# Sigmoid attention and an ELU feed-forward layer: weights by tile of the hidden layer, whole stores, and block sums made earlier

## The chip, the cores and the metric

One core of a Trainium2 chip runs the whole kernel. The metric is the time of one execution on the device, in microseconds (us). Three executions of the kernel before took 1148.48, 1149.53 and 1149.55 us; the median is 1149.53.

## The reference

For 8 batches of 448 tokens and 12 heads of width 64, everything in float32:

```python
scores = q @ k.T / sqrt(64) - log(448)
x = (sigmoid(scores) @ v)            # heads side by side: 3584 tokens x 768
h = x @ w_in                         # 768 -> 2048
g = where(h > 0, h, exp(min(h, 0)) - 1)
out = g @ w_out                      # 2048 -> 768
```

## The kernel before, in words

**Number format.** A float32 operand is scaled by a power of two and split into two float16 parts, a high and a low one. A product is three float16 matmuls (high by high, high by low, low by high). Batches 0 and 1 have their attention in float32 and their first layer from the split parts of `w_in`.

**Batches 2 to 7** compute the first layer by a seven-product scheme on 2 x 2 blocks. Its operands are the four blocks of `w_in` and four sums of them, for each of eight units of two f tiles (an f tile is 128 of the 2048 hidden columns). They are made once, on the chip, by `sums_of_parts` (L340), which is a generator: `make_sums` (L418) asks it for one step. A unit takes seven steps: two that add high and low parts to full numbers (DVE, L394) and store blocks "11" and "12"; one with two block additions (DVE, L352) that stores "22"; one with two more additions and the high half of a sum (ACT, L364); three that make a low half (DVE, L368), store it, and make the next high half. The last low half of a unit falls into the first step of the next. All eight units are 57 steps. The results rest in three rotating buffers of a tile `room` and are written to a DRAM tensor `blend` by POOL's DMA queue (L420, `store_sums`). Blocks that need no new scale (six of the eight units) are written straight from `w_in`'s parts `wi`, each in two DMAs, one for the high and one for the low part; for the other two units ACT rescales them first (L386). `room` uses the same memory as `xh`, the first layer's input of batch 2.

**The weights.** `wi` holds for each unit the parts as (high or low, row tile c, 256 columns): an f tile of one c is a run of 128. Its memory becomes, when a unit's sums are made, the ring of ten blocks that the later batches load from `blend` on SP's queue (`load_block`, L955).

**Order of the work.** The schedule is written by hand: program order is the order on each engine. The first stage follows a list of tokens; 21 of them (`K`) are steps of the sums. Then comes the first layer of batch 1 (`moe1`): behind each of its 16 f tiles `beside_first` (L1489) runs what `order` lists, 15 steps of the sums in all. For each batch b from 2 on, a loop over six pairs of heads (numbered 0 to 5 here) mixes scores and sigmoid of pair n (PE to ACT, L681; ACT L692 and DVE L693 split the result), values of pair n-1 (PE), and matmuls of the second layer of batch b-1 (`fill`, L1115) that keep PE at work. `scale_next` takes the next pair's scales from PE through DVE (L195 and following) to POOL (L591, L594); `split_next` then splits the next pair's q and k with these scales (ACT L620, DVE L623) and its v (ACT L209, DVE L210) and issues the loads of a later pair; `measure_next` starts the maxima of another. In batch 2, sums' steps stand at four or five places of a pair, 20 in all, and one call in pair 4 runs all that are left. Behind pair 5 comes the first layer by blocks (`moe1_blocks`, L969): 28 products of 18 matmuls. Each of the two running sums A and B gets a PSUM bank; `bank` issues one matmul of ones into a new bank, then ACT copies a product into it (L1064, L1074) and later products accumulate there. Behind product n `order_of_blocks` has steps of the next pair; those at 18, 19, 20 and 23 are the four steps of one `split_next`. The last two halves of g are left over (`left_of_g`) and are made beside pair 0 of the next batch, or, behind batch 7, at once.

**The end.** The second layer of batch 7 runs alone: 2 halves of four tiles of tokens (48 matmuls each); the fourth of each half holds 64 tokens of batch 6 and 64 of batch 7 and is written by two DMAs.

Of the kernel before, what the change touches and what calls it, by code (L numbers as in the profile page):

```python
# [10 lines left out]
BF16 = mybir.dt.bfloat16  # L11
# [54 lines left out]
def attention_ffn(  # L66
# [9 lines left out]
    nc = tc.nc  # L76
# [46 lines left out]
    wi = space.rearrange("p (u h c x) -> p u h c x", u=NU, h=2, c=NK)  # L123
# [3 lines left out]
    def part(at, n, dt=F16):  # L127
# [4 lines left out]
        "p (n j c h x) -> p n j c h x", n=RING, j=2, c=HK, h=2  # L132
# [147 lines left out]
    def w_in_parts(u):  # L280
# [28 lines left out]

        def lower():  # L310
# [12 lines left out]
            "E": lambda: nc.scalar.mul(d[:, 0], st["t"], s()),  # L323
# [16 lines left out]
    def sums_of_parts():  # L340
# [4 lines left out]
        full = full.rearrange("p (c x) -> p c x", c=NK)  # L345

        def block(t, x):
            c, f = HK * (x[1] == "2"), P * (x[0] == "2")
            return t[:, c : c + HK, f : f + P]
# [6 lines left out]
        def next_out():  # L356
            nonlocal out
            out += 1
            t = room[:, 4 + out % 3]
            return t, t.rearrange("p (c h x) -> p h c x", c=HK, h=2)  # L360
# [16 lines left out]
        def copy(x, slot):  # L377
            w, j = divmod(u, 2)
            if j or u in ALIKE:
                dst = blend[w, slot].rearrange("p (j c h x) -> p j h c x", j=2, c=HK, h=2)  # L380
                for h in range(2):
                    unsent.append((dst[:, j, h], block(wi[:, NU - 1 - u, h], x)))
                return
            t = next_out()
            for h in range(2):
                nc.scalar.mul(t[1][:, h], block(wi[:, NU - 1 - u, h], x), r)  # L386
            store(t, slot)

        for u in (0, 1, 2, 3, 7, 6, 5, 4):
            r = wt[:, u * WF : u * WF + 1]  # L390
            parts = wi[:, NU - 1 - u]
            for i in range(2):
                c = slice(i * HK, (i + 1) * HK)
                nc.vector.tensor_tensor(full[:, c], parts[:, 0, c], parts[:, 1, c], op=ALU.add)  # L394
# [495 lines left out]
    def moe1_products(b, f):  # L890
# [6 lines left out]
        for c in range(NK):  # L897
            for wj, xj in ((0, 0), (0, 1), (1, 0)):
                nc.tensor.matmul(  # L899
                    ph[:, :S], wi[:, NU - 1 - f // WF, wj, c, f % WF * P :][:, :P], hidden_of(b, c)[:, xj],  # L900
# [54 lines left out]
    def load_block(n):  # L955

        b, i = divmod(n, len(USES))
        if b < B - WHOLE:
            k, w = USES[i]
            nc.sync.dma_start(  # L960
                ring[:, n % RING].rearrange("p j c h x -> p (j c h x)"),
# [3 lines left out]
    def moe1_blocks(b, g, m, behind_first, first, beside):  # L965
# [14 lines left out]
        def bank(k, w):  # L980
# [6 lines left out]
            if name not in sums:  # L987
                t = ps.tile([P, 2, 512], F32, tag="psc", name=f"{name}{b}", bufs=2)
                sums[name] = t[:, 0]
                nc.tensor.matmul(  # L990
                    t[:, 0, :S], ones, xh[:, 0].rearrange("p h x -> p (h x)").bitcast(BF16)[:, :S],
                    start=True, stop=True, skip_group_check=True,
                )
            return sums[name][:, :S]

        def product(k, w):
# [3 lines left out]
            for j in range(2):  # L1000
                n = 0
                for c in range(HK):
                    for wj, xj in ((0, 0), (0, 1), (1, 0)):
                        nc.tensor.matmul(  # L1004
                            to[:, j * HS : (j + 1) * HS], block[:, j, c, wj], rhs(k, c, xj),
# [97 lines left out]
        nc.scalar.activation(warm, bias, AF.Sigmoid)  # L1103
# [541 lines left out]
```

## Time and profile before

| | |
|---|---|
| Median of three executions | 1149.53 us |
| The profiled execution | 1147.72 us, span 1145.9 us |
| PE busy | 1113.4 us (97%) |
| DVE busy | 815.5 us (71%) |
| ACT busy | 768.1 us (67%) |
| POOL busy | 131.7 us |
| Granted TensorE clock | 0.998 over the span |

The span is from the first to the last instruction of the profiled execution; the time has some 1.8 us around it. PE's busy share counts matmuls that overlap in the array, so it is read together with the idle time ahead of single matmuls: `[2.35 <-ACT sg L681]` behind a row says that the engine sat idle for 2.35 us before it and that ACT's instruction of line 681 ended that. PE is matmuls, PEld their weight loads, DVE VectorE, ACT ScalarE, POOL GpSimd, SP SyncE.

### The profile page before, as it was taken

What the parts mean: (1) busy time and instruction counts of PE and PEld (TensorE: products, weight loads), DVE (VectorE), ACT (ScalarE), POOL (GpSimd) and SP (SyncE); (2) the same over time, 40 slices, a digit from 0 to 9 for tenths busy, and PEclk for the clock granted to TensorE, in tenths of its full rate; (3) what the DMA queues carried; (4) which work ended last, traced back from release to release, by engine and by line L of the source; (5) the groups of instructions that cost most, each with busy time, mean ns of one, the idle gap of its engine ahead of it and who ended that gap; (6) DMA issues with size and microseconds to landing.
All of it is one profiled execution on the core that took longest, in us unless ns stands there. A gap on an engine that the chain in (4) does not pass through costs nothing.

```text
span 1145.9 us, 22290 instructions
## 1 busy us (share of the span) xinstructions
PE 1113.4 (97%) x8626; PEld 715.9 (62%) x8626; DVE 815.5 (71%) x1681; ACT 768.1 (67%) x1080; POOL 131.7 (11%) x351
## 2 busy tenths in 40 slices
PE   6899999999999999999999999999999999999998
PEld 2333455555545985579555895569655796559864
DVE  2989899787995768876786567876786567874500
ACT  4998887477765578767866468776766568775600
POOL 0000011334540001100010001100010000110000
PEclk9999999999999999999999999999999999999999
DMA  9983743334773683538542594429553285417100
GB/s 240 256 241 75 235 122 114 131 83 108 185 192 111 197 277 73 117 114 265 139 114 55 129 286 115 111 70 293 151 120 84 65 281 157 97 45 213 35 23 28
DMA packets 224666, 164.65 MB, mean 144 GB/s; under 512 B 170384, under 2 KB 189840, under 8 KB 224560
## 3 DMA queue, kind: packets, MB, share of 16 engines
q1 hardware_dynamic: 220400, 152.22, 48.4%
q0 software_dynamic: 4160, 11.01, 3.0%
q8 instruction: 67, 1.10, 0.4%
q14 instruction: 39, 0.32, 0.1%
HBM read 124.65 MB, written 22.02 MB: 128 GB/s over the span
## 4 chain that ended last, share of the span: by engine, by line
PE 71%; ACT 13%; DVE 8%; DMA 5%; issue 3%; SPq 1%; POOL 0%; ACTq 0%; DVEq 0%; POOLq 0%
PE po L1115 23%; PE X L1004 11%; PE ph L899 7%; PE psc L657 7%; PE pav L706 6%; PE po_r L1115 5%; PE Y L1004 3%; PE A L1004 3%; ACT sg L681 3%; PE B L1004 2%; ACT g L1030 1%; DMA raw<-in_q_dram 1%; PE pav L724 1%; DVE at L693 1%; DMA blend<-room 1%
## 5 line engine op out<-in xcount | busy, mean ns | idle before, releaser
L1115 PE MATMUL po<-wo,g 128*128 128x384 f16 x2304 | 387.8, 327 | 1.3 <-DVE g L1036 1.3
L1115 PEld LDWEIGHTS <-g 128*128 128x128 f16 x2688 | 257.6, 98 | 187.1 <-issue 18.5
L1004 PEld LDWEIGHTS <-wi 128*128 128x128 f16 x3024 | 288.3, 98 | 6.4 <-issue 4.6
L693 DVE SCALAR_TENSOR_TENSOR at<-sg,at 128x896 f16<-128x896 f32 x126 | 132.4, 1087 | 54.0 <-ACT at L692 54.0
L681 ACT ACTIVATE sg<-psc,bias,sc 128x896 f32<-128x896 f32 x108 | 114.8, 1091 | 42.7 <-PE psc L657 36.1
L1004 PE MATMUL X<-wi 128*128 128x224 f16 x1296 | 133.0, 259 | 1.5 <-DVE c L1051 1.5
L657 PE MATMUL psc<-qk 64*128 64x448 f16 (+2 forms) x960 | 108.5, 376 | 7.7 <-ACT sg L681 7.7
L692 ACT ACTIVATE at<-sg 128x896 f16<-128x896 f32 x126 | 113.4, 945 | 0.6
L899 PE MATMUL ph<-xh,wi 128*128 128x448 f16 x576 | 110.9, 352 | 0.0
L620 ACT ACTIVATE nat<-raw,sc 128x384 f16<-128x384 f32 (+1 forms) x108 | 51.3, 534 | 69.2 <-POOL sc L591 66.7
L899 PEld LDWEIGHTS <-wi 128*128 128x128 f16 x576 | 55.9, 98 | 53.0 <-issue 1.4
L591 POOL TENSOR_SCALAR sc<-sc 128x3 f32<-128x3 f32 x36 | 10.9, 303 | 605.2 <-DVE xs L551 432.5
L706 PE MATMUL pav<-at,vn 128*64 128x448 f16 x648 | 68.2, 355 | 0.0
L657 PEld LDWEIGHTS <-qk 64*128 64x128 f16 (+1 forms) x864 | 31.1, 97 | 56.0 <-issue 39.5
L1115 PE MATMUL po_r<-wo,g 128*128 128x384 f16 x384 | 64.3, 326 | 0.0
L1019 DVE SCALAR_TENSOR_TENSOR eb<-eb,c 128x896 f32<-128x896 f32 x24 | 26.2, 1091 | 49.9 <-ACT c L1016 49.9
L1125 DVE TENSOR_SCALAR o<-po,osc 128x384 f32<-128x384 f32 x48 | 29.3, 611 | 38.4 <-PE po L1115 37.6
L623 DVE SCALAR_TENSOR_TENSOR nat<-raw,sc,nat 128x384 f16<-128x384 f32 (+1 forms) x108 | 50.8, 525 | 7.0 <-ACT nat L620 7.0
L706 PEld LDWEIGHTS <-vn 128*64 128x64 f16 x648 | 33.6, 109 | 32.1 <-issue 13.0
L1004 PE MATMUL X<-xh,wi 128*128 128x224 f16 x432 | 45.4, 259 | 0.0
L1004 PE MATMUL Y<-xh,wi 128*128 128x224 f16 x432 | 45.3, 259 | 0.0
L1004 PE MATMUL B<-xh,wi 128*128 128x224 f16 x432 | 45.3, 259 | 0.0
(176 smaller groups left out, 1512.6 us busy)
## 6 DMA issues: line engine op xcount, KB each, us to landing
wi<-blend SPq DMA_DIRECT2D x168, 384.0 KB, 4.6
stage<-in_moe_w_in_dram SPq DMA_DIRECT2D x8, 1536.0 KB, 7.7
wo<-in_moe_w_out_dram SPq DMA_DIRECT2D x13, 768.0 KB, 4.8
raw<-in_q_dram SPq DMA_DIRECT2D x96, 96.0 KB, 3.4
raw<-in_k_dram SPq DMA_DIRECT2D x96, 96.0 KB, 3.1
out_dram<-o SPq DMA_DIRECT2D x48, 192.0 KB, 1.9
blend<-room POOLq DMA_DIRECT2D x38, 192.0 KB, 2.6
rv<-in_v_dram SPq DMA_DIRECT2D x36, 192.0 KB, 2.7
```

Source lines behind the costliest of these rows:

```text
L620: nc.scalar.mul(hi, src, s)
L623: nc.vector.scalar_tensor_tensor(lo, src, s, hi, op0=ALU.mult, op1=ALU.subtract)
L657: nc.tensor.matmul(psc[:, j, :S] if g < NC else psc[rows[x], j, :S], kk[rows[j], o], qq[rows[j], :S], start=(n == 0), stop=(n == n_parts - 1),
L681: nc.scalar.activation(sg, psc[:, :, :S], AF.Sigmoid, bias=bias, scale=scale)
L692: nc.scalar.mul(parts[0], sg, 2.0**ATOP)
L693: nc.vector.scalar_tensor_tensor(parts[1], sg, 2.0**ATOP, parts[0], op0=ALU.mult, op1=ALU.subtract)
L706: nc.tensor.matmul(pav[rows[j], :S], vv[i][:, j * NC + g if g < NC else 2 * NC + j], sg[k][:, j], start=(g == 0 and n == 0), stop=False,)
L899: nc.tensor.matmul(ph[:, :S], wi[:, NU - 1 - f // WF, wj, c, f % WF * P :][:, :P], hidden_of(b, c)[:, xj], start=(n == 0), stop=(n == 3 * ...
L1004: nc.tensor.matmul(to[:, j * HS : (j + 1) * HS], block[:, j, c, wj], rhs(k, c, xj), start=(k in (1, 5) and j == 0 and n == 0), stop=(j == ...
L1019: nc.vector.scalar_tensor_tensor(e, e, -1.0, src, op0=ALU.add, op1=ALU.min)
L1115: nc.tensor.matmul(po[:, :HM], lh(gj, f), wo[:, i, f, wj], start=(n == 0), stop=(n == 3 * NF - 1),)
L1125: nc.vector.tensor_scalar(o, po[:, :HM], sc, None, op0=ALU.mult)
```

## The change

- `wi` lies by f tile: (high or low, f tile, c, 128 columns), so a block of one f tile and three c is one run. ACT's split of `w_in` (L323) reads its source in that order; DVE's low half (L311) becomes two instructions, one for each f tile. Blocks in `blend` and the ring are ordered (high or low, c) in place of (c, high or low).
- A plain block is stored in one DMA where there were two, and rescaled by one ACT instruction where there were two.
- The matmul of ones into the banks of A and B goes.
- Steps of the sums: in batch 1's first layer 20 in place of 15; in batch 2's pairs 16 (four in each of pairs 0 to 3) in place of 20 and the call for the rest. With 21 in the first stage that is 57.
- In pair 0 of every batch `scale_next` stands ahead of the splits of the first two sigmoid tiles, in place of behind them.
- The last step of the second `split_next` in `moe1_blocks` (the split of v and the next loads) moves from product 23 to product 25.
- Behind batch 7 ACT's sigmoid table isn't loaded.
- In the last half of batch 7's second layer the tile of two batches comes first in place of last.

```diff
-    wi = space.rearrange("p (u h c x) -> p u h c x", u=NU, h=2, c=NK)
+    wi = space.rearrange("p (u h f c x) -> p u h f c x", u=NU, h=2, f=WF, c=NK)
...
         def lower():
-            nc.vector.scalar_tensor_tensor(
-                d[:, 1], st["t"], s(), d[:, 0], op0=ALU.mult, op1=ALU.subtract
-            )
+            for i in range(WF):
+                nc.vector.scalar_tensor_tensor(
+                    d[:, 1, i], by_tile()[:, i], s(), d[:, 0, i], op0=ALU.mult, op1=ALU.subtract
+                )
...
-            "E": lambda: nc.scalar.mul(d[:, 0], st["t"], s()),
+            "E": lambda: nc.scalar.mul(d[:, 0], by_tile(), s()),
...
         def copy(x, slot):
             w, j = divmod(u, 2)
+            c, f = HK * (x[1] == "2"), int(x[0] == "2")
+            src = wi[:, NU - 1 - u, :, f, c : c + HK]
             if j or u in ALIKE:
-                dst = blend[w, slot].rearrange("p (j c h x) -> p j h c x", j=2, c=HK, h=2)
-                for h in range(2):
-                    unsent.append((dst[:, j, h], block(wi[:, NU - 1 - u, h], x)))
+                dst = blend[w, slot].rearrange("p (j h c x) -> p j h c x", j=2, h=2, c=HK)
+                unsent.append((dst[:, j], src))
                 return
             t = next_out()
-            for h in range(2):
-                nc.scalar.mul(t[1][:, h], block(wi[:, NU - 1 - u, h], x), r)
+            nc.scalar.mul(t[1], src, r)
             store(t, slot)
...
                 sums[name] = t[:, 0]
-                nc.tensor.matmul(
-                    t[:, 0, :S], ones, xh[:, 0].rearrange("p h x -> p (h x)").bitcast(BF16)[:, :S],
-                    start=True, stop=True, skip_group_check=True,
-                )
...
-        nc.scalar.activation(warm, bias, AF.Sigmoid)
+        if b < B - 1:
+            nc.scalar.activation(warm, bias, AF.Sigmoid)
...
-            for c in range(NC + j):
+            tiles = list(range(NC + j))
+            if b == B - 1 and i == NH - 1:
+                tiles.insert(0, tiles.pop())
+            for c in tiles:
...
-    order = {1: [scale_next], 3: [split_next], 4: [measure_next, make_sums], 6: [scale_next, make_sums], 8: [split_next], 10: [make_sums] * 2, 12: [make_sums] * 2, 14: [measure_next, make_sums]}
+    order = {1: [scale_next, make_sums], 3: [split_next, make_sums], 4: [measure_next, make_sums], 6: [scale_next, make_sums], 8: [split_next, make_sums], 10: [make_sums] * 2, 12: [make_sums] * 2, 13: [make_sums] * 2, 14: [measure_next, make_sums], 15: [make_sums] * 2}
...
-        16: scale_next, 18: split_step, 19: split_step, 20: split_step, 23: split_step,
+        16: scale_next, 18: split_step, 19: split_step, 20: split_step, 25: split_step,
...
+                if hp == 0:
+                    scale_next()
                 for t in range(2):
                     p.halves(t)
                 store_sums()
-                if hp == 0:
-                    scale_next()
-                if b == 2 and hp < NP - 1:
+                if b == 2 and hp < NP - 2:
                     make_sums()
...
-                if b == 2 and hp < NP - 1:
+                if b == 2 and hp < NP - 2:
                     make_sums()
-                if b == 2 and hp == HK + 1:
-                    make_sums(8 * NF)
...
-                elif b == 2 and prep and hp:
-                    make_sums()
```

## Rows read from the trace of the kernel before

**Rows 1.** Windows: us, busy us (x instructions) by engine, clock, DMA share, GB/s.
```profile
28.00:57.00 29.00, 25.67 (x154) 10.24 (x152) 27.00 (x57) 27.21 (x28) 0.00 (x0) 1.00 0.91 255
222.00:277.00 55.00, 55.00 (x296) 28.35 (x295) 43.70 (x106) 37.40 (x79) 18.14 (x35) 1.00 0.40 107
```

**Rows 2.** Groups by line and form, PE: count | busy us, mean ns | idle, releaser.
```profile
L1115 PE MATMUL po<-wo,g 128*128 128x384 f16 x2304 | 387.8, 327 | 1.3 <-DVE g L1036 1.3
...
L1004 PE MATMUL X<-wi 128*128 128x224 f16 x1296 | 133.0, 259 | 1.5 <-DVE c L1051 1.5
...
L657 PE MATMUL psc<-qk 64*128 64x448 f16 x648 | 74.8, 351 | 6.5 <-ACT sg L681 6.5
...
L657 PE MATMUL psc<-qk 64*64 64x448 f16 x216 | 13.9, 359 | 1.2 <-ACT sg L681 1.2
...
L990 PE MATMUL A<-xh,ones 128*128 128x448 bf16 x6 | 2.1, 353 | 0.0
```

**Rows 3.** Timeline of PE, batch 2's first layer begins: start us, us, instruction.
```profile
372.79 0.35 PE L990 MATMUL A<-xh,ones 128*128 128x448 bf16 x1
372.98 1.30 PE L1115 MATMUL po_r<-wo,g 128*128 128x384 f16 x7
```

**Rows 4.** Timeline, batch 3, from pair 0 to pair 1.
```profile
436.90 0.16 DVE L195 TENSOR_REDUCE al<-pb 128x3 f32<-128x12 f32 x1
...
437.84 1.07 DVE L693 SCALAR_TENSOR_TENSOR at<-sg,at 128x896 f16<-128x896 f32 x1
...
438.02 0.62 ACT L620 ACTIVATE nat<-raw,sc 128x384 f16<-128x384 f32 x1 [0.59 <-POOL sc L591]
438.05 1.12 POOL L594 COPY sc<-sc 64x1 f32<-64x1 f32 x2
...
439.21 0.91 ACT L620 ACTIVATE nat<-raw,sc 128x128 f16<-128x128 f32 x2 [0.56 <-POOL sc L594]
...
441.76 0.74 PE L657 MATMUL psc<-qk 64*128 64x448 f16 x6 [0.79 <-ACT sg L681]
```

**Rows 5.** Timeline, batch 2, pairs 2 to 5.
```profile
324.90 0.61 ACT L364 ACTIVATE room<-room,wt 128x384 f16<-128x384 f32 x1 [1.15 <-DMA blend<-room]
...
326.55 0.74 PE L657 MATMUL psc<-qk 64*128 64x448 f16 x6 [2.35 <-ACT sg L681]
...
355.75 0.67 ACT L804 ACTIVATE xh<-wi,xs 128x448 f16<-128x448 f32 x1 [7.95 <-DMA blend<-room]
...
357.98 0.74 PE L657 MATMUL psc<-qk 64*128 64x448 f16 x6 [1.78 <-ACT sg L681]
```

**Rows 6.** Groups by line and form, the sums' instructions and a split.
```profile
L364 ACT ACTIVATE room<-room,wt 128x384 f16<-128x384 f32 x32 | 19.3, 609 | 22.5 <-DVE room L352 11.2 <-DMA blend<-room 10.4 <-ACT g L209 0.9
L368 DVE SCALAR_TENSOR_TENSOR room<-room,wt 128x384 f16<-128x384 f32 x32 | 19.3, 613 | 2.8 <-ACT room L364 2.8
...
L352 DVE TENSOR_TENSOR room<-room 128x384 f32<-128x384 f32 x32 | 17.8, 555 | 0.7
...
L475 ACT ACTIVATE wo<-wo,swo 128x384 f16<-128x384 f32 x28 | 15.8, 612 | 5.2 <-DVE swo L501 3.7 <-DVE wo L481 1.5
L394 DVE TENSOR_TENSOR room<-wi 128x768 f32<-128x768 f16 x16 | 14.9, 951 | 0.0
```

**Rows 7.** Timeline, end of batch 2's first layer: the split of v on DVE.
```profile
418.82 0.75 DVE L210 SCALAR_TENSOR_TENSOR vn<-rv,sc,vn 128x512 f16<-128x512 f32 x1
```

**Rows 8.** Timeline, behind batch 7's first layer.
```profile
1081.22 1.28 ACT L1103 ACT_TABLE_LOAD   x1
...
1084.89 2.29 PE L1115 MATMUL po<-wo,g 128*128 128x384 f16 x13 [0.69 <-DVE g L1036]
```

**Rows 9.** Timeline, the end of the span.
```profile
1141.97 1.12 SPq L1127 DMA_DIRECT2D out_dram<-o_r  x2
```

**Rows 10.** DMA issues: count, KB each, median us to landing.
```profile
out_dram<-o SPq DMA_DIRECT2D x48, 192.0 KB, 1.9
...
out_dram<-o_r SPq DMA_DIRECT2D x16, 96.0 KB, 2.2
```

More of the change, by code (lines that the diff above doesn't have):

```diff
@@ L131, in attention_ffn @@
     ring = part(0, RING * BLOCK).rearrange(
-        "p (n j c h x) -> p n j c h x", n=RING, j=2, c=HK, h=2
+        "p (n j h c x) -> p n j h c x", n=RING, j=2, h=2, c=HK
     )
@@ L308, in s, with by_tile @@
             return w_in_scales[u + (u in ALIKE)]
+        def by_tile():
+            return st["t"].rearrange("p c (f x) -> p f c x", f=WF)
         def lower():
-            nc.vector.scalar_tensor_tensor(
-                d[:, 1], st["t"], s(), d[:, 0], op0=ALU.mult, op1=ALU.subtract
-            )
+            for i in range(WF):
+                nc.vector.scalar_tensor_tensor(
+                    d[:, 1, i], by_tile()[:, i], s(), d[:, 0, i], op0=ALU.mult, op1=ALU.subtract
+                )
         return {
@@ L344, in sums_of_parts @@
         full = room[:, :4].rearrange("p b x -> p (b x)").bitcast(F32)
-        full = full.rearrange("p (c x) -> p c x", c=NK)
+        full = full.rearrange("p (f c x) -> p f c x", f=WF, c=NK)
         def block(t, x):
-            c, f = HK * (x[1] == "2"), P * (x[0] == "2")
-            return t[:, c : c + HK, f : f + P]
+            c, f = HK * (x[1] == "2"), int(x[0] == "2")
+            return t[:, f, c : c + HK]
         def add(x, y, z, op):
@@ L359, in next_out @@
             t = room[:, 4 + out % 3]
-            return t, t.rearrange("p (c h x) -> p h c x", c=HK, h=2)
+            return t, t.rearrange("p (h c x) -> p h c x", c=HK, h=2)
         def high(x):
@@ L393, in sums_of_parts @@
                 c = slice(i * HK, (i + 1) * HK)
-                nc.vector.tensor_tensor(full[:, c], parts[:, 0, c], parts[:, 1, c], op=ALU.add)
+                nc.vector.tensor_tensor(
+                    full[:, :, c], parts[:, 0, :, c], parts[:, 1, :, c], op=ALU.add
+                )
                 copy("12" if i else "11", 4 + i)
@@ L899, in moe1_products @@
                 nc.tensor.matmul(
-                    ph[:, :S], wi[:, NU - 1 - f // WF, wj, c, f % WF * P :][:, :P], hidden_of(b, c)[:, xj],
+                    ph[:, :S], wi[:, NU - 1 - f // WF, wj, f % WF, c], hidden_of(b, c)[:, xj],
                     start=(n == 0), stop=(n == 3 * NK - 1),
@@ L960, in load_block @@
             nc.sync.dma_start(
-                ring[:, n % RING].rearrange("p j c h x -> p (j c h x)"),
+                ring[:, n % RING].rearrange("p j h c x -> p (j h c x)"),
                 blend[w, PRODUCTS[k][0]],
@@ L1004, in product @@
                         nc.tensor.matmul(
-                            to[:, j * HS : (j + 1) * HS], block[:, j, c, wj], rhs(k, c, xj),
+                            to[:, j * HS : (j + 1) * HS], block[:, j, wj, c], rhs(k, c, xj),
                             start=(k in (1, 5) and j == 0 and n == 0),
```

1 line of the change is left out of this document (added).

## The prediction

> **What bounds the kernel now.** I read the windows first. In batch 1's first layer PE has work for 55.00 of 55.00 us, DVE for 43.70 and ACT for 37.40 [rows 1]: PE sets the pace. In the first stage's stretch from 28 to 57 us DVE has 27.00 and ACT 27.21 of 29.00 us [rows 1]: there the two of them set it. The later batches are again PE's, so an edit is worth what it takes out of PE's own work or out of the idle time ahead of a matmul, provided no later wait gives that back. The groups by line say how much idle time there is: scores (psc) waited 6.5 + 1.2 us for the sigmoid, the second layer's matmuls (po) 1.3 us for DVE's half of g, block products (X) 1.5 us for DVE's sum c [rows 2]. The timelines say where each of these lies; they are taken up with the edit that they belong to.
>
> **The change part by part.** All sums are made against the profiled execution, 1147.72 us; the median of the three runs is 1149.53, 1.81 above it, and I add that at the end.
>
> *The matmuls of ones.* A's six [rows 2], and as many for B, go: two in each of six batches. One starts at 372.79 and the next matmul at 372.98 [rows 3], though each is busy for 0.35: they overlap, and what one costs PE is 0.19. PE stands in its own queue there and nothing else is late: 12 x 0.19 = -2.3 us. ACT's copy into the bank no longer waits for PE; ACT gains nothing that anyone waits for.
>
> *scale_next ahead of the splits in pair 0.* In batch 3 DVE first works through two splits (the third, at 437.84, takes 1.07 us) and only then starts the scales at 436.90; POOL's copies of them run from 438.05 for 1.12 us, and ACT, which has nothing else, stands 0.59 and 0.56 us ahead of the splits of q and k [rows 4]. Behind these on ACT's queue are the split of v and pair 1's first two sigmoids, and for these PE waits 0.79 us at 441.76 [rows 4] and once more some 0.24 us for the second tile. The 6.5 us of scores are 2.35 + 1.78 of batch 2 [rows 5] and three times 0.79, so batches 3, 5 and 7 have this wait; the 1.2 us are five second waits of 0.24 [rows 2]. Ahead of the splits the scales start 2.0 us earlier. ACT can give up 0.59 + 0.56 = 1.15 us, more than the 0.79 + 0.24 = 1.03 that PE lacks. Upper end 3 x 1.03 = 3.1; lower end 0, if POOL's copies are held up by the splits that now run beside them. In these rows that happens already: the copies (438.05 to 439.17) lie beside the split of 437.84 to 438.91 [rows 4]. One split's length each (1.05 us) would take some 2.1 us for two copies, 1.0 more than now, and still leave 1.0 of the 2.0. I take -2.8. The two splits are 0.9 us later for it; the values of pair 0 that read them are matmuls of pair 1, several us on.
>
> The Trainium skill has a rule that speaks against this edit ("SBUF — State Buffer", Who interferes with whom): a DVE instruction with two SBUF inputs and a GpSimd instruction that reads SBUF lock each other out for a whole instruction. The split has two such inputs, so by the rule each copy may wait for a whole split; the row's long copies agree. By the rule's worst case (three splits in a row get in first) the 2.0 us are used up and this term is about 0; that is the first rival.
>
> *Sums' steps.* Batch 2 has two places where they hold PE up. At 324.90 ACT waits 1.15 us for a store before it may write a `room` buffer (L364, 0.61 us), with pair 3's first sigmoids queued behind; PE then waits 2.35 us and some 0.25 [rows 5]. At 355.75 ACT has stood for 7.95 us ahead of L804, until the last store has released the memory that `xh` takes over; PE waits 1.78 us and 0.24 [rows 5]. With five steps more in batch 1 the 57 end at the end of pair 3 in place of the middle of pair 4. Two pairs take 31.4 us (326.55 to 357.98), so the last store goes out about a third of a pair, 5 us, earlier; ACT's 7.95 shrink to some 3, and the 1.78 + 0.24 us of PE are less than these 5. The second place goes: -2.0 (at worst -1.5). At the first, steps 46 to 49 are replaced by 50 to 53: one low half, two sums of parts, four additions, one high half whose buffer has long been stored. The 1.15 us go. But DVE has 0.61 + 2 x 0.95 + 4 x 0.56 = 4.7 us of them where it had 2 x 0.56 + 3 x 0.61 = 2.9 [rows 6]; against that pair 1, which had five steps (4.8 us), has 46 to 49 (2.9 us). So DVE comes about 1.9 us earlier into pair 2 and loses it again there, and the scales, in the middle of it, are no later than now. Between 2.6 and, if the same wait turns up at the end of pair 1 (step 49's high half stands there now, behind the store of step 47), 0: I take -1.9.
>
> What is added in batch 1 (steps 37 to 41): one sum of parts, four additions, three high and two low halves: DVE 0.95 + 4 x 0.56 + 2 x 0.61 = 4.4 us, ACT 3 x 0.61 = 1.8 us [rows 6]. DVE has 11.3 us free in that window and ACT 17.6 [rows 1], so PE hides them. Only at the seam, where the table is loaded for the first sigmoid of batch 2, one high half more stands ahead of it: +0.3, between 0 and its 0.61. POOL's stores go with their steps; plain ones are half as many, and nobody but ACT's next buffer waits for POOL.
>
> *The weights' layout.* DVE's low half is two instructions for each of eight units. From 384 to 768 columns DVE goes from 0.56 to 0.95 us [rows 6], so an instruction has about 0.16 of its own: at most 8 x 0.16 = 1.3 us, in a stretch where DVE and ACT set the pace [rows 1]; most of the eight overlap with something, +0.4 (0 to 1.3). ACT's strided source is free by the nearest rows: L364 reads three separate runs of 128 in 0.609 us, L475 one run of 384 in 0.612 [rows 6]. The single stores and the single rescaling take work from POOL, DMA and ACT where none of them is waited for: 0.
>
> *The split of v from product 23 to 25.* It lies on DVE at 418.82 for 0.75 us [rows 7], ahead of the sum c for which the last X product waits: 1.5 us over the run, five batches with 0.3 each [rows 2] (the last batch has no next pair). That wait goes. But DVE's work for the other half of c now has the split ahead of it, and ACT's chain from c through the last exponentials, the table load and the first sigmoid ends in the half of g for which po waits in the same batches (1.3 less batch 7's 0.69, [rows 2, 8]). PE comes there earlier and waits longer; what it gained is given back. SP's loads go two products later with it, past two loads of blocks; both are for work a batch or a pair on. I take 0, between -1.5 (the chain has room) and +3.8 (five times 0.75, the split wholly in the chain).
>
> *Behind batch 7.* ACT loads a table for 1.28 us [rows 8] ahead of the half of g for which PE stands 0.69 us at 1084.89 [rows 8]. Without it ACT is ready before PE: -0.8 (0.7 to 1.0, since the idle time is counted from the end of matmuls that overlap).
>
> *The last tile.* Two issues take 1.12 us, so the second starts about 0.55 us behind the first [rows 9], and lands after 2.2 us where one store of a whole tile needs 1.9 [rows 10]: -0.8, between -0.3 and -0.9.
>
> Sum: -2.3 - 2.8 - 2.0 - 1.9 + 0.3 + 0.4 + 0 - 0.8 - 0.8 = -9.9. The profiled execution would be 1137.8, the median 1139.6.
>
> **The rivals.**
> 1. *POOL stays the last.* The copies wait for the three splits of pair 0, and ACT's idle time remains. For it: the copies in rows 4 take 1.12 us beside one split. Against: they need to lose all of 2.0 us. Time 1139.6 + 2.8 = 1142.4.
> 2. *The wait moves.* Batch 2's pair 2 keeps its stall or hands it to pair 1, whose last step now has a high half behind a fresh store. For it: ACT waited 10.4 us for such stores in all [rows 6]. Against: pair 1's store is sent earlier in the pair. Time 1139.6 + 1.9 + 1.0 = 1142.5.
> 3. *The split of v lies in the chain.* Each layer's seam is up to 0.75 us longer. For it: ACT's chain is what po waits for already. Against: DVE was late by the same split before. Time 1139.6 + 3.8 = 1143.4. With the other two: 1148.1, no difference.
> 4. *The seam has room*, and the 1.5 us are kept, the other terms at their upper ends: 1136.2.
> 5. *Slower: the new order of `w_in` in the first stage.* From 28 us on ACT has 1.8 and DVE 2.0 of 29 us free [rows 1], so what a strided source costs there is paid in full. It decides from 12.2 us on (9.9 to eat up, 2.3 to be seen), which is 1.5 us for each of eight units on one engine: a read at half speed (1536 columns, 4 x 0.40 = 1.6) would be 12.8, the time 1152.4. Against: L364 and L475 [rows 6].
>
> **How the numbers follow.** Forecast as above 0.52; rival 1 0.13, rival 2 0.13, rival 3 0.10, of these 0.04 together with the others; rival 4 0.07; rival 5 0.05. The time is the forecast's, 1139.6. The range reaches over rivals 1 to 3 one at a time and down to rival 4: 1136.0 to 1144.0. 0.2% is about 2.3 us, what a measurement here can tell from no change: faster 0.91, the same 0.04 (the three together), slower 0.05.
>
> **What would show it.** No instruction of L990's kind; scores' idle time down from 7.7 to under 2 us, none of it in batches 3, 5 and 7; no wait of ACT's L804 over 4 us; X no longer waiting for c, and po's wait for g grown by as much; batch 7's 0.69 gone; one store at the end. Wrong would be: idle time of psc in pair 1 of the odd batches as before, a new wait in batch 2's pair 1, ACT's L323 over 2 us (rival 5), or ph in batch 1 waiting for ACT.

## The result and the profile after

The changed kernel takes 1137.47 us (median of 4 runs, 1134.91 to 1137.94) beside 1149.54 us of the kernel before in the same session (4 runs): a ratio of 0.9897, 95% interval 0.9876 to 0.9918. It is 12.1 us faster; 9.9 were forecast, and 1137.47 lies in the range of 1136.0 to 1144.0. The profiled execution took 1137.94 us (span 1136.14), where the sum gave 1137.8. That closeness is partly luck: two terms were off by about 2 us in opposite directions, and the first stage, which differs between executions of one kernel, moved by 1.5 us more than its term.

The groups of PE after, as in [rows 2] (L1118, L1006 and L663 were L1115, L1004 and L657); the matmuls of ones (L990) are gone:

```profile
L1118 PE MATMUL po<-wo,g 128*128 128x384 f16 x2304 | 386.4, 326 | 2.3 <-DVE g L1038 2.3
L1006 PE MATMUL X<-wi 128*128 128x224 f16 x1296 | 133.0, 259 | 0.4
...
L663 PE MATMUL psc<-qk 64*128 64x448 f16 x648 | 74.8, 351 | 0.4
...
L663 PE MATMUL psc<-qk 64*64 64x448 f16 x216 | 13.7, 357 | 0.2 <-ACT sg L687 0.2
```

The scores' 7.7 us of idle time have become 0.6, X's 1.5 have become 0.4, and po's 1.3 have grown to 2.3 although batch 7's 0.69 [rows 8] are no longer among them.

The timeline of batch 3 from pair 0 to pair 1, as in [rows 4]:

```profile
430.52 0.16 DVE L195 TENSOR_REDUCE al<-pb 128x3 f32<-128x12 f32 x1
...
431.46 3.08 DVE L699 SCALAR_TENSOR_TENSOR at<-sg,at 128x896 f16<-128x896 f32 x3
431.69 1.90 POOL L600 COPY sc<-sc 64x1 f32<-64x1 f32 x2
432.98 1.55 ACT L626 ACTIVATE nat<-raw,sc 128x384 f16<-128x384 f32 x3
433.47 1.31 PE L663 MATMUL psc<-qk 64*128 64x448 f16 x12
```

All three splits (L699) now stand behind the scales; ACT goes through its three steps without a wait, and PE's scores wait for nothing. POOL's two copies are longer beside the splits: 1.90 us, where they took 1.12. Each of the two ends some 0.04 us behind the end of a split (432.58 behind 432.54, 433.58 behind 433.54); the median of all such copies in this profile is 0.18 us.

ACT at batch 2's stores, as in [rows 5], with L368 for L364 and L810 for L804:

```profile
310.62 0.61 ACT L368 ACTIVATE room<-room,wt 128x384 f16<-128x384 f32 x1 [0.36 <-DMA blend<-room]
324.56 0.60 ACT L368 ACTIVATE room<-room,wt 128x384 f16<-128x384 f32 x1
...
336.61 0.61 ACT L368 ACTIVATE room<-room,wt 128x384 f16<-128x384 f32 x1 [1.91 <-DMA blend<-room]
347.14 0.67 ACT L810 ACTIVATE xh<-wi,xs 128x448 f16<-128x448 f32 x1 [1.36 <-DMA blend<-room]
359.17 1.23 ACT L810 ACTIVATE xh<-wi,xs 128x448 f16<-128x448 f32 x2
```

The waits of 1.15 and 7.95 us are gone from their places. Three shorter ones (0.36, 1.91 and 1.36 us) stand at other places, and in this execution PE has no idle time of over 0.25 us in batch 2's pairs. Behind batch 7's first layer and at the end, as in [rows 8, 9]:

```profile
1069.79 8.45 PE L1118 MATMUL po<-wo,g 128*128 128x384 f16 x51
```

```profile
1133.04 0.33 SPq L1130 DMA_DIRECT2D out_dram<-o  x1
```

po runs 51 matmuls in a row where it stood 0.69 us, and one store is issued where there were two.

To see where the time went I cut every profiled execution at the starts of PE's matmuls: "first" is up to the first matmul of batch 1's layer, "att b" from the last block product of batch b-1 (for batch 2: from the last matmul of batch 1's layer) to the first of b, "lay b" from the first to the last block product of b, "second" batch 7's second layer, "end" what follows its last matmul. All in us. Batch 1's layer, not shown, takes 54.4 us in every kernel, with 15 steps of the sums or with 20, so PE hides the steps added there. Lay 3, 5 and 6, not shown either, agree with lay 2 and 4 within 0.1, but for lay 5 of before, e6 and e9 (0.3 longer).

```
kernel                first  att2  lay2  att3  att4  lay4  att5  att6  att7  lay7 second end
before               222.18 94.48 51.62 73.78 88.13 51.61 73.51 88.12 73.51 51.06 63.66 4.66
after                224.08 88.45 51.17 72.96 88.64 51.17 72.96 88.63 72.96 50.68 62.66 3.78
after again (e11)    223.26 89.96 51.13 72.95 88.63 51.12 72.93 88.62 72.94 50.68 62.66 3.78
sums back (e1)       224.30 92.09 51.14 72.95 88.62 51.13 72.95 88.63 72.95 50.68 62.66 3.77
scale_next back (e2) 224.99 88.59 51.14 74.01 88.63 51.14 74.01 88.63 74.01 50.68 62.66 3.77
v at 23 (e3)         222.78 88.62 51.61 72.45 88.12 51.61 72.68 88.12 72.45 50.68 62.66 3.79
layout alone (e4)    227.07 95.63 51.61 73.51 88.13 51.60 73.51 88.12 73.51 51.06 63.66 4.62
ones back (e5)       224.19 88.65 51.15 72.96 88.63 51.15 72.95 88.63 72.95 51.06 62.66 3.78
ones alone (e9)      221.95 96.18 51.60 73.78 88.12 51.58 73.50 88.12 73.50 50.68 63.65 4.65
two tiles (e6)       221.34 88.68 51.15 78.15 88.03 51.15 78.30 88.03 76.62 50.68 62.66 3.79
two of next (e10)    220.61 89.34 51.13 72.94 88.02 51.13 72.94 88.03 72.95 50.68 62.66 3.78
```

From before to after: batch 2's attention -6.0, batches 3, 5 and 7 -0.8, -0.55 and -0.55, batches 4 and 6 +0.5 each, five layers -0.45 each (batch 5's -0.7), batch 7's -0.4, the second layer -1.0, the end -0.9, the first stage +1.9: -9.8 us, as the spans say (1145.95 and 1136.14).

One loss in batch 2 stands in no column of idle time. Windows of the kernel before, behind its wait at 326.55 [rows 5], and of the kernel after at the same place; the columns are those of [rows 1], the clock is the third from the right:

```profile
318.00:324.00 6.00, 6.00 (x49) 3.08 (x47) 5.27 (x16) 2.03 (x4) 2.74 (x8) 1.00 0.73 235
328.05:331.40 3.35, 3.35 (x18) 1.45 (x11) 3.35 (x5) 3.35 (x5) 0.54 (x1) 0.50 0.58 158
331.40:337.40 6.00, 6.00 (x40) 3.57 (x39) 5.63 (x13) 2.41 (x4) 4.99 (x9) 1.00 0.92 253
```

```profile
328.00:331.40 3.40, 3.40 (x23) 2.05 (x22) 3.26 (x9) 2.31 (x3) 0.00 (x0) 1.00 0.83 178
```

After PE of the kernel before had stood 2.35 us and, one tile on, 0.25 us, the granted clock was 0.50 (1.2 GHz) for 3.4 us, from 328.0 to 331.4, and PE was "busy" through all of it. Half of 3.4 us is 1.7 us of lost work that no idle column counts, and the starts of matmuls agree: po's follow each other every 0.32 us in this stretch and every 0.16 us behind it.

### The profile page after: what moved, and what is told of

The parts are those of the page before. It is cut to its first block, busy times and chain, and to the rows that moved or that the text cites. A ratio compares the mean times of both kernels' runs of the same rounds, so it can differ in the third digit from the quotient of the medians.

```text
span 1136.1 us, 22252 instructions
## 1 busy us (share of the span) xinstructions
PE 1108.8 (98%) x8614; PEld 713.6 (63%) x8614; DVE 815.6 (72%) x1689; ACT 765.3 (67%) x1072; POOL 119.4 (11%) x333
## 4 chain that ended last, share of the span: by engine, by line
PE 68%; ACT 13%; DVE 10%; DMA 5%; issue 2%; SPq 1%; POOL 0%; DVEq 0%; ACTq 0%; POOLq 0%
PE po L1118 27%; PE X L1006 8%; PE psc L663 7%; PE pav L712 7%; PE ph L905 7%; PE po_r L1118 5%; PE Y L1006 2%; ACT sg L687 2%; PE A L1006 2%; PE B L1006 2%; ACT g L1032 2%; DMA wi<-blend 2%; PE pav L730 1%; DVE g L1038 1%; ACT eb L1017 1%
## 5 line engine op out<-in xcount | busy, mean ns | idle before, releaser
L1118 PE MATMUL po<-wo,g 128*128 128x384 f16 x2304 | 386.4, 326 | 2.3 <-DVE g L1038 2.3
L1118 PEld LDWEIGHTS <-g 128*128 128x128 f16 x2688 | 257.3, 98 | 185.9 <-issue 16.8
L1006 PEld LDWEIGHTS <-wi 128*128 128x128 f16 x3024 | 288.2, 98 | 5.3 <-issue 4.4
L699 DVE SCALAR_TENSOR_TENSOR at<-sg,at 128x896 f16<-128x896 f32 x126 | 132.0, 1086 | 55.3 <-ACT at L698 55.3
L1006 PE MATMUL X<-wi 128*128 128x224 f16 x1296 | 133.0, 259 | 0.4
L663 PE MATMUL psc<-qk 64*128 64x448 f16 (+2 forms) x960 | 108.0, 375 | 0.6 <-ACT sg L687 0.2
L1118 PE MATMUL po_r<-wo,g 128*128 128x384 f16 x384 | 64.1, 326 | 0.0
L663 PEld LDWEIGHTS <-qk 64*128 64x128 f16 (+1 forms) x864 | 30.6, 97 | 49.2 <-issue 31.3
L629 DVE SCALAR_TENSOR_TENSOR nat<-raw,sc,nat 128x384 f16<-128x384 f32 (+1 forms) x108 | 50.8, 525 | 7.1 <-ACT nat L626 6.7
L687 ACT ACTIVATE sg<-psc,bias 128x896 f32<-128x896 f32 x42 | 41.3, 1012 | 6.4 <-PE psc L663 6.3
L1006 PE MATMUL X<-xh,wi 128*128 128x224 f16 x432 | 45.4, 259 | 0.0
L1006 PE MATMUL B<-xh,wi 128*128 128x224 f16 x432 | 45.3, 259 | 0.0
```

What stands on the lines that cost most here:

```text
L629: nc.vector.scalar_tensor_tensor(lo, src, s, hi, op0=ALU.mult, op1=ALU.subtract)
L663: nc.tensor.matmul(psc[:, j, :S] if g < NC else psc[rows[x], j, :S], kk[rows[j], o], qq[rows[j], :S], start=(n == 0), stop=(n == n_parts - 1),
L687: nc.scalar.activation(sg, psc[:, :, :S], AF.Sigmoid, bias=bias, scale=scale)
L699: nc.vector.scalar_tensor_tensor(parts[1], sg, 2.0**ATOP, parts[0], op0=ALU.mult, op1=ALU.subtract)
L1006: nc.tensor.matmul(to[:, j * HS : (j + 1) * HS], block[:, j, wj, c], rhs(k, c, xj), start=(k in (1, 5) and j == 0 and n == 0), stop=(j == ...
L1118: nc.tensor.matmul(po[:, :HM], lh(gj, f), wo[:, i, f, wj], start=(n == 0), stop=(n == 3 * NF - 1),)
```

## The experiments

Eleven experiments, in three sessions; in these the kernel before took 1148.57 (e1 to e4), 1148.96 (e5 to e8) and 1148.72 us (e9 to e11), and each ratio is to it. One of them (e11) is the changed kernel once more, unedited, for the spread of a single kernel.

**e11, the changed kernel again.**

> The changed kernel itself, unedited, on the same chip as the runs beside it, for what two executions of one kernel differ by. Theory: the stages from batch 1's layer on repeat within 0.1 us each (they are set by the order of the instructions), and what two executions differ by lies in the first stage (up to batch 1's layer at 222 to 227 us in the profiles so far), where inputs land and half-clock stretches come or do not; median 1136.5 to 1138.5. Rival: the later stages differ as much between executions, and then differences of 1 us between stages of two kernels tell nothing.

1135.74 us (1133.87 to 1138.28), ratio 0.9887 (0.9862 to 0.9911), 0.8 us below the range expected. Of the stages the theory holds with one exception: all stages from batch 2's layer on repeat within 0.1 us, the first stage differs by 0.8, and batch 2's attention by 1.5. ACT's timeline of e11 shows the place:

```profile
311.59 0.61 ACT L368 ACTIVATE room<-room,wt 128x384 f16<-128x384 f32 x1 [2.15 <-DMA blend<-room]
```

```profile
313.24 0.74 PE L663 MATMUL psc<-qk 64*128 64x448 f16 x6 [1.59 <-ACT sg L687]
```

This high half waited 0.36 us for its buffer's store in the first profile and 2.15 us in this one, and the scores of pair 2 behind it waited 1.59 us. In the other profiles with the new places PE stands there between 0 (e2) and some 1.3 us (e7), from start to start. So differences of up to 1.5 us in batch 2's attention tell nothing by themselves.

**e1, sums' steps back at their old places.**

```diff
-    order = {1: [scale_next, make_sums], 3: [split_next, make_sums], ...}
+    order = {1: [scale_next], 3: [split_next], ...}
...
-                if b == 2 and hp < NP - 2:
+                if b == 2 and hp < NP - 1:
                     make_sums()
+                if b == 2 and hp == HK + 1:
+                    make_sums(8 * NF)
...
+                elif b == 2 and prep and hp:
+                    make_sums()
```

> The changed kernel with the sums' steps where they were before (15 in batch 1, 20 and the call for the rest in batch 2); all else as changed. My theory: the steps' places alone made batch 2 shorter, so the two waits of PE for the sigmoid (some 2.6 and 2.0 us) come back, with the stretch of half clock behind the first: 5.0 to 6.5 us slower than the changed kernel, about 1143. Rival: it was the single stores and the earlier scales of pair 0 that relieved batch 2; then it is at most 1.5 us slower, about 1138.5, and batch 2's pairs take 88 to 90 us, not 93 or more.

1142.08 us, ratio 0.9942 (0.9930 to 0.9954). Both waits are back, PE's in e1:

```profile
327.73 0.74 PE L663 MATMUL psc<-qk 64*128 64x448 f16 x6 [1.50 <-ACT sg L687]
...
357.68 0.74 PE L663 MATMUL psc<-qk 64*128 64x448 f16 x6 [1.94 <-ACT sg L687]
```

Batch 2's attention is 92.09 us, 3.6 over the changed kernel's profile and 2.1 over e11's; no other stage from there on differs. The clock stayed at 1.00 behind both waits, so this is their price without the half-clock stretch, and the stretch that the theory had behind the first is not in this execution. The times lie further apart, 0.9942 for the changed kernel's 0.9897 and e11's 0.9887, which is 5 to 6 us; of that the profile shows 3.6 us at most in batch 2, and where the rest lies in the executions that were not profiled is open. The rival, which had at most 1.5 us and 88 to 90 us for batch 2, falls.

**e2, scale_next back behind the splits.**

```diff
-                if hp == 0:
-                    scale_next()
                 for t in range(2):
                     p.halves(t)
                 store_sums()
+                if hp == 0:
+                    scale_next()
```

> The changed kernel with scale_next behind the first two splits in pair 0, as before. My theory: in batches 3, 5 and 7 PE waits for the sigmoid in pair 1 again, 0.8 and 0.24 us each: 3.0 to 3.5 us slower than the changed kernel, about 1140.7; batches 2, 4 and 6 within 0.5 us. Rival: the waits went since PE now reaches the block layer's seam at another time; then it is within 0.7 us.

1140.03 us, ratio 0.9925 (0.9910 to 0.9940). Batches 3, 5 and 7 are 74.01 us each in place of 72.96: 1.05 times three is 3.15 us, and no other stage behind the first moves. The wait is the old one to the hundredth, PE's in e2, batch 3, beside [rows 4]:

```profile
438.40 0.74 PE L663 MATMUL psc<-qk 64*128 64x448 f16 x6 [0.79 <-ACT sg L687]
439.39 0.76 PE L663 MATMUL psc<-qk 64*64 64x448 f16 x12 [0.24 <-ACT sg L687]
```

**e3, the split of v back at product 23.**

```diff
-        16: scale_next, 18: split_step, 19: split_step, 20: split_step, 25: split_step,
+        16: scale_next, 18: split_step, 19: split_step, 20: split_step, 23: split_step,
```

> The changed kernel with the split of v behind product 23, as before. My theory (given back at the seam): X's wait of 0.3 us returns in five batches, and the second layer's wait for g, 0.63 us in the changed kernel, shrinks by as much or more: within 0.8 us of the changed kernel, 1136.7 to 1138.3. Rival that the seam had room: 1.5 to 2.3 us slower, about 1139.5. Rival that the split now lies in ACT's chain: 1.5 to 3.8 us faster, about 1135.

1136.53 us, ratio 0.9890 (0.9871 to 0.9908): no difference from the changed kernel. PE's groups of e3 show the exchange:

```profile
L1118 PE MATMUL po<-wo,g 128*128 128x384 f16 x2304 | 386.3, 326 | 0.5 <-DVE g L1038 0.5
L1006 PE MATMUL X<-wi 128*128 128x224 f16 x1296 | 132.9, 259 | 1.9 <-DVE c L1053 1.5
```

X's wait for c is back (1.5 us), po's wait for g has shrunk from 2.3 to 0.5. In the table each of five layers is 0.45 us longer and the attention that follows 0.3 to 0.5 shorter; from batch 2's first block product to the last matmul e3 is 0.2 us shorter.

**e4, the kernel before with the layout alone** (the strided order of `w_in`, the single copies, two low halves for each unit).

```diff
-    wi = space.rearrange("p (u h c x) -> p u h c x", u=NU, h=2, c=NK)
+    wi = space.rearrange("p (u h f c x) -> p u h f c x", u=NU, h=2, f=WF, c=NK)
...
-            nc.vector.scalar_tensor_tensor(
-                d[:, 1], st["t"], s(), d[:, 0], op0=ALU.mult, op1=ALU.subtract
-            )
+            for i in range(WF):
+                nc.vector.scalar_tensor_tensor(
+                    d[:, 1, i], by_tile()[:, i], s(), d[:, 0, i], op0=ALU.mult, op1=ALU.subtract
+                )
```

> The kernel before with the layout alone: parts by f tile, two instructions for a low half, plain blocks stored and rescaled whole. My theory: 0 to 0.6 us slower than before, about 1149.8; the first stage's 1.9 us in the changed kernel's trace were input loads that landed later in that execution. Rival A: the 1.9 us are the layout's, 1151.4. Rival B: fewer stores relieve batch 2, 2 us faster, 1147.5.

1147.09 us (1143.78 to 1153.13), ratio 0.9990 (0.9975 to 1.0005): not to be told from nothing. The profile alone would mislead: its execution was the longest, 1153.13 us, with a first stage of 227.07 us and a wait of 3.76 us at 362.36 in batch 2, behind which the clock was 0.50 for 3.4 us. But the eleven profiles with the new layout have first stages from 220.6 to 227.1 us, and the two with the old one 221.95 and 222.18, in the midst of them. What the strided order costs each engine stands in ACT's high halves of `w_in`, before and after, and in DVE's low halves after (1812 ns before, for both f tiles in one):

```profile
L323 ACT ACTIVATE wi<-stage,swi x8: 1563/1578/1647, 35.4 to 107.8; 128x1536 f16<-128x1536 f32 x8
```

```profile
L327 ACT ACTIVATE wi<-stage,swi x8: 1562/1580/1610, 34.9 to 108.6; 128x1536 f16<-128x1536 f32 x8
L315 DVE SCALAR_TENSOR_TENSOR wi<-stage,swi,wi x16: 1009/1012/1017, 40.7 to 111.6; 128x768 f16<-128x768 f32 x16
```

The columns are the shortest, median and longest in ns. ACT's read is free (1578 and 1580 ns); DVE's two instructions take 2 x 1012 = 2024 ns, 0.21 us more for each of the eight units.

**e9, the kernel before without the ones matmuls, and e5, the changed kernel with them.** The same lines, taken out of the one and put into the other:

```diff
-                nc.tensor.matmul(
-                    t[:, 0, :S], ones, xh[:, 0]...,
-                    start=True, stop=True, skip_group_check=True,
-                )
```

> The changed kernel with one part undone: the ones matmul that opened each sums bank stands again, once in each of the six block layers. Theory (the prediction's term): TensorE runs in order and is busy 98% of the span, so what it no longer has to do is gained whole: about 0.39 us for each of six, 2.3 us in all; ratio to the kernel before about 0.992 (1139.8 where the changed kernel has 1137.5), each block layer 0.39 us longer from its first matmul to its last. Rival: the matmul stands ahead of product 7's first block and hides a wait that comes there anyway; then the time stays within 0.5 us of the changed kernel (ratio 0.9895 or less) and the layer's length is the same.

> The kernel before with one part of the change alone: the ones matmuls gone. The prediction's term: 0.39 us in each of six block layers, 2.3 us, ratio 0.998 (1146.7 where the kernel before has 1149.0), block layers of 51.23 us instead of 51.62. Rival, from the run in which they were put back: these layers go at the pace of the copies and sums that free X's banks, and what TensorE no longer does it then waits, for c and for the copies of A and B: five layers stay at 51.6 us (with new X waits of 0.15 to 0.28 us, 0.45 a layer), only batch 7's, which has no splits beside it, is 0.38 us shorter; the ratio is not to be told from 1.

e5: 1139.01 us, ratio 0.9914 (0.9901 to 0.9928). e9: 1148.24 us, ratio 0.9992 (0.9978 to 1.0007). By the stages the theory is wrong in five of the six layers, and the rivals hold there. With and without ones, the layers of batches 2 to 6 have the same length (e9 51.60 and before 51.62; e5 51.15 and after 51.17); only batch 7's is 0.38 shorter without them (51.06 and 50.68). e9's time agrees with its rival. e5's doesn't: 0.9914 lies nearer to the theory's 0.992 than to the rival's 0.9895, though its interval overlaps the changed kernel's (0.9876 to 0.9918). Its profiled execution is only 0.5 us longer than the changed kernel's, 0.38 of it in batch 7's layer; where its other executions lost more is not known. X's groups of e5 and of e9:

```profile
L1010 PE MATMUL X<-wi 128*128 128x224 f16 x1296 | 133.0, 259 | 0.0
```

```profile
L1000 PE MATMUL X<-wi 128*128 128x224 f16 x1296 | 133.0, 259 | 2.1 <-DVE c L1047 1.7
```

With ones, e5's X waits for nothing; without them the changed kernel's X waits 0.4 us. Counted from start to start, batch 2's layer of e9 has X waits of 0.15 us (behind c) and 0.27 us (behind ACT's copy into B's bank) where the kernel before has 0.06 us at the second place and none at the first: 0.36 us more, about the 0.38 us that two ones matmuls cost. Batch 7's layer, with no splits beside it, loses nothing.

Batch 2's attention is longer in e9 (96.18 us, 94.48 before), though the edit doesn't touch it. PE's second wait there and the window behind it:

```profile
358.15 2.38 PE L657 MATMUL psc<-qk 64*128 64x448 f16 x18 [2.28 <-ACT sg L681]
```

```profile
358.40:361.80 3.40, 3.40 (x23) 1.11 (x20) 3.40 (x6) 3.40 (x5) 0.00 (x0) 0.50 0.18 60
```

In this execution the second wait was 2.28 us, in the first profile 1.78 [rows 5], and here the half clock follows it too. Up to the end of batch 2's attention the two kernels have the same instructions, so one such stretch in the one execution and two in the other are a spread between executions.

**e6 and e8, two tiles of the second layer side by side** (f 0 to 11 of both, then f 12 to 15 of both; e8 with the split of v at 23 as well).

```diff
+            if b >= WHOLE and i == 0:
+                two = [tile_of(c, i) for c in tiles[:2]]
+                for n in (NF - 4, 4):
+                    for t in two:
+                        for _ in range(n):
+                            next(t)
+                            yield
+                tiles = tiles[2:]
```

> The changed kernel with one addition: in the batches whose second layer is filled into the next batch's attention, the first two of its tiles run side by side, f 0 to 11 of the one, f 0 to 11 of the other, then f 12 to 15 of each, so that the parts of g that come last are wanted 36 matmuls (5.9 us) later. Theory: po's waits for g in the changed kernel (0.625 us in each of five batches) are gone and nothing else is late in the next 5 us: 3.1 us less, ratio to the kernel before about 0.987 (1134.4). Rival: the wait is only passed on to the scores of the next pair (their bank is freed by ScalarE, which still has the same work in the same order): the po wait goes, but psc's idle grows by as much and the ratio stays at 0.9895.

> The kernel with the two tiles side by side, and the split of v back at step 23 where the kernel before had it. Theory: the split of v costs one of two waits: at 23, X waits 0.46 us for c in five layers, at 25, po waits for g. With the wait at po covered by the other tile, 25 is the better place: this run comes 2.3 us after the one with 25 (1136.7 where that has 1134.4). Rival: the place of the split moves nothing: both within 0.7 us.

1152.36 and 1152.34 us, ratios 1.0036 (1.0023 to 1.0048) and 1.0040 (1.0023 to 1.0057): 15 us slower than the changed kernel, which neither the theories nor the rival of e6 had. PE, then DVE, of e6 in batch 3:

```profile
437.32 1.62 PE L1118 MATMUL po<-wo,g 128*128 128x384 f16 x9
442.61 4.60 PE L1118 MATMUL po<-wo,g 128*128 128x384 f16 x18 [3.67 <-DVE o L1128]
```

```profile
439.94 2.09 DVE L699 SCALAR_TENSOR_TENSOR at<-sg,at 128x896 f16<-128x896 f32 x2 [1.06 <-ACT at L698]
441.95 0.61 DVE L1128 TENSOR_SCALAR o<-po,osc 128x384 f32<-128x384 f32 x1
```

po has two banks. Run side by side, both tiles end close together, and the third has to wait until DVE has copied the first one out, which it does only behind four splits of the next pair. The same 3.67 us stand in batches 3, 5 and 7, in e8 as in e6, and with the first two goes a stretch at a clock of 0.50; these stages of e6 are 5.2, 5.3 and 3.7 us longer. In batch 3:

```profile
442.35:445.70 3.35, 3.09 (x10) 1.43 (x10) 2.46 (x11) 2.02 (x4) 1.52 (x6) 0.50 0.19 65
```

Batches 4 and 6 have no such wait and show the gain that was meant (88.03 for 88.63). As for the split of v, e8's layers are 0.45 longer and its attentions only 0.24 to 0.5 shorter; the times don't tell the two apart, as e8's rival had it.

**e10, only two f of the second tile ahead of the first tile's last four.**

```diff
+                for t, n in ((0, NF - 4), (1, 2), (0, 4), (1, NF - 2)):
+                    for _ in range(n):
+                        next(two[t])
+                        yield
```

> The changed kernel with the first tile of the second layer run to f 11, then two f of the second tile (6 matmuls, 0.98 us), then f 12 to 15 of the first, and the rest of the second. Theory: po's wait for the last low part of g (0.625 us in batches 3 to 7) is covered by these 0.98 us, and as the first tile ends only 1 us later than in the changed kernel, its bank is copied out in time for the third tile (6.9 us of the second tile lie between, where the two tiles side by side left 2.0): 3.1 us less in the stages from batch 3 to 7, time about 1134.4, ratio 0.987. Rival 1: the wait for the bank (DVE o, 3.84 us at three places in the run with two tiles side by side) is there again, and the run is slower than the changed kernel. Rival 2: the 0.625 us come back at psc of the next pair; the time stays at the changed kernel's.

1134.49 us, ratio 0.9878 (0.9855 to 0.9902), beside e11's 1135.74 in the same session: the lowest time of the study, though the intervals overlap. That it is the 1134.4 of the theory is luck: by the stages the theory holds in batches 4 and 6 only (-0.6 each), 1.2 us of its 3.1, and rival 2 in batches 3, 5 and 7 (0). PE's groups of e10, and its scores in batch 3:

```profile
L1118 PE MATMUL po<-wo,g 128*128 128x384 f16 x2304 | 385.6, 326 | 0.0
...
L663 PE MATMUL psc<-qk 64*128 64x448 f16 x648 | 74.9, 352 | 1.8 <-ACT sg L687 1.6
```

```profile
433.54 0.74 PE L663 MATMUL psc<-qk 64*128 64x448 f16 x6 [0.20 <-ACT sg L687]
434.52 0.76 PE L663 MATMUL psc<-qk 64*64 64x448 f16 x12 [0.24 <-ACT sg L687]
```

po waits for nothing any more. Of psc's idle time in this form, 1.8 us for 0.4, 0.97 us is batch 2's wait, as in e11. In the odd batches pair 1 now waits 0.20 us and, in the form of 64 by 64, 0.24 us, together about the 0.46 us that po waited there in the changed kernel, so ACT, which was what pair 1 waited for before the change, is again the last.

**e7, a probe of the clock.** In the changed kernel ACT is kept busy with copies that nobody reads ahead of pair 3's sigmoids, a different number in each batch.

```diff
+                if hp == 3 and b > 2:
+                    for _ in range({3: 8, 5: 13, 7: 18, 4: 21, 6: 26}[b]):
+                        nc.scalar.copy(ones_in, ones)
```

> A probe of the half-clock stretch, not a version: in the changed kernel ScalarE is made late ahead of the sigmoids of pair 3 by 8, 13, 18, 21 and 26 small copies of about 0.3 us (batches 3, 5, 7, 4 and 6), so that TensorE stands idle for five different times before its next scores. Theory: a row of waits of about 2.5 us or more on TensorE is followed by 3.4 us at a granted clock of 0.50 (as behind the 2.35 us in batch 2 of the kernel before), which costs about 1.7 us on top of the idle time, and the shorter ones are followed by none. Rival: the stretch in batch 2 of the kernel before came at that place by chance and the stretches do not go with the idle times: then no idle time here, or as often a short one as a long one, is followed by it.

1157.76 us, one run. PE's waits (four of the five), and the windows behind all five:

```profile
460.95 0.74 PE L663 MATMUL psc<-qk 64*128 64x448 f16 x6 [0.87 <-ACT sg L687]
...
591.60 0.74 PE L663 MATMUL psc<-qk 64*128 64x448 f16 x6 [2.14 <-ACT sg L687]
...
731.96 0.74 PE L663 MATMUL psc<-qk 64*128 64x448 f16 x6 [2.52 <-ACT sg L687]
...
1007.78 2.57 PE L663 MATMUL psc<-qk 64*128 64x448 f16 x18 [4.17 <-ACT sg L687]
```

```profile
461.80:465.20 3.40, 3.26 (x29) 1.88 (x29) 2.09 (x2) 3.40 (x5) 0.00 (x0) 1.00 0.55 121
593.10:596.40 3.30, 3.30 (x18) 1.36 (x11) 2.09 (x2) 3.30 (x5) 0.00 (x0) 0.50 0.29 68
733.00:736.30 3.30, 3.30 (x19) 1.40 (x19) 2.10 (x2) 3.30 (x4) 0.00 (x0) 0.50 0.56 137
866.10:869.50 3.40, 3.40 (x23) 1.10 (x20) 1.82 (x2) 3.40 (x5) 0.00 (x0) 0.50 0.05 14
1006.10:1012.80 6.70, 5.02 (x26) 1.87 (x26) 2.09 (x2) 6.67 (x9) 0.00 (x0) 0.50 0.01 2
```

The four long waits (the one not shown is 3.79 us) go with the half clock and the short one doesn't. With the wait of 4.17 us it stood for twice as long as with the others, from 1006.0 on, when PE had already stood 2.4 us. The rival falls, and of the theory its 2.5 us, since 2.14 us were followed by it too. Nor does each long wait have it: in e6 and e8 the same wait of 3.67 us went with the half clock in batches 3 and 5 and with a clock of 1.00 in batch 7.

## Why the prediction came out right

**The bound.** PE's own chain of work, with the waits in it, set the time of everything behind the first stage; each gain and each give-back was read as a wait of PE's, and one part, the half clock in batch 2, that the prediction didn't have.

**The matmuls of ones: -2.3 forecast, -0.4 measured.** The step that failed is "PE stands in its own queue there and nothing else is late". What a matmul cost PE was right (0.19), but five of the six layers are held to their pace by DVE's c and ACT's copy into B's bank. [Rows 2] had X waiting for c, which should have warned me: where one wait in a loop is real, the next ones may be just covered. The term holds only in batch 7's layer.

**scale_next: -2.8 forecast, -3.15 measured** (e2). The estimate of some 2.1 us for two copies beside the splits came near (1.90), and it left enough of the 2.0 us, so rival 1 is out. The Trainium skill's rule ("SBUF — State Buffer", Who interferes with whom) holds here, one split for each copy: each ends some 0.04 us behind the end of a split, and the two take 0.8 us more than before.

**Sums' steps: -2.0 and -1.9 forecast, -4.4 in idle time in the profiled pair, and 1.7 more from the clock.** From start to start PE's waits in batch 2 fall from 5.3 us (2.5 + 0.4 + 1.95 + 0.4) to 0.9 (0.17 at the seam, 0.28 + 0.41 within pair 3). The second place went as said. Mis-sized was the first: its 2.35 us had also cost the clock, which I hadn't read behind the wait. With the steps alone undone (e1) batch 2 lost 3.6 us, or 2.1 from e11's, without a stretch at half clock. Rival 2 holds in part: the wait for a fresh store came up in pair 1's step, and cost PE from 0 to some 1.7 us depending on the execution; with it the stage gained 4.5 in place of 6.0. The kernels with the old places spread as well, 92.09 to 96.18 us with none, one or two stretches at half clock, so the gain in the median isn't settled to better than some 2 us, nor is the price of rival 2.

**The seam: +0.3 forecast**; psc waits 0.17 us at 285.75. **The layout: +0.4 forecast**; below what e4 can show (-2.9 to +0.6 us). DVE's second instruction costs it 0.21 us for each unit, 1.7 in all, where the prediction had 0.16 and at most 1.3; how much of that reaches the time is not shown. ACT's strided read took 1580 ns for 1578, so rival 5, 12.2 us and more, is out.

**The split of v: 0 forecast, 0.2 measured** (e3). The mechanism is as described: the wait for c goes (-0.45 in each of five layers) and po's wait for g grows by as much. Rivals 3 and 4 are out. (Where the prediction puts the first three rivals together, its terms add up to 1149.1, not 1148.1: 1139.6 + 2.8 + 2.9 + 3.8. The chances don't change by that.)

**Behind batch 7 -0.8, the last tile -0.8**: -1.0 and -0.9. No run undoes either alone, but the two stages are 62.66 and 3.8 us in each kernel of the table that has both edits and 63.7 and 4.6 in each that has neither.

Together the terms behind the first stage were forecast at -10.3 us and came to -11.7 in the profile (-10.5 in e11): 1.9 lost with ones, and 2.4 more than forecast gained in batch 2 (0.9 in e11). The first stage came out 1.9 longer in the profiled pair, which e4 and the spread of the eleven profiles put down to the execution, not to the edit. The median fell further than the profiled execution, 12.1 us for 9.8: the 1.81 us that I added for the median of the kernel before were a spread between its executions and didn't carry over.

## What to carry to other kernels

An instruction taken off the busiest engine is worth its time only in the stretches where no other engine's copy or sum keeps the same pace; look there for the next wait, however small, and test the removal by itself. Read the granted clock behind each of TensorE's waits of a few us: the wait of 2.35 us cost 1.7 us on top. Two tiles side by side to cover an input's lateness need the banks to be free as well as the input; a short overlap (two steps of the second tile) was enough.

## What the runs showed of the hardware

The half-clock stretches were not expected. All of PE's waits of over 1 us from batch 2 on, in the thirteen profiles, with the granted clock that went with them:

| PE stood (us) | granted clock |
|---|---|
| 1.18 to 1.94 (six waits) | 1.00 |
| 2.14, 2.28, 2.30, 2.35, 2.52, 3.76, 3.79 | 0.50 (1.2 GHz) for 3.4 us, then 1.00 |
| 3.67, six times | 0.50 for 3.4 us in batches 3 and 5 of e6 and e8; 1.00 in batch 7 of both |
| 4.17 | 0.50 for 6.8 us, then 1.00 |

Why batch 7's waits of 3.67 us differ from the four others is open. In the first stage such stretches came in four executions (from 193.4 us in e1, from 50.8 and 194.2 in e2, from 196.7 in e4, from 52.3 in e5), and these have the four longest first stages (224.2 to 227.1 us; 220.6 to 224.1 in the nine others, after and e11 among them). What decides there was not tried.

POOL's copies of 64 x 1 took 0.18 us in the median of the changed kernel's profile, and 0.89 to 0.97 us in pair 0 of batches 3 to 7, where each ended 0.04 to 0.05 us behind the end of one of DVE's splits.
